# Two infini-attention and dense layers on one core: tile 3's statistics, tile 0's evacuation, the order of the first k and q products, and beta's load

## The chip, the cores and the metric

The kernel runs on one core of a Trainium2 chip. The engines of that core are TensorE (PE, matmuls, with PEld for its weight loads), VectorE (DVE), ScalarE (ACT), GpSimd (POOL) and SyncE (SP, which here only issues DMAs). The metric is the time of one execution in microseconds (us); less is better.

## The reference

A block of two layers is applied twice to a sequence `x` of 2048 tokens with 640 features, in bf16:

```python
x = x + _A_ref(_layernorm(x), wq, wk, wv, wo, beta)
x = x + _B_ref(_layernorm(x), w1, w2)      # relu(x @ w1) @ w2, 1728 hidden features
x = x + _A_ref(_layernorm(x), wq, wk, wv, wo, beta)
x = x + _B_ref(_layernorm(x), w1, w2)
```

The attention `_A_ref` has 32 heads of 20 features and cuts the sequence into four segments of 512 tokens. In each segment a causal softmax attention is computed within the segment, and a linear attention reads a memory `M` with a normaliser `z`; the two are mixed by a gate per head:

```python
g = _sigmoid(beta)
p = _softmax(q k^T * scale + mask)
o = g * (phi(q) M) / (phi(q) z + 1e-6) + (1 - g) * p v
M, z = M + phi(k)^T v, z + sum(phi(k))
```

## The kernel before

The sequence is held in SBUF as 16 tiles of 128 tokens (`x_sb`); a segment `s` is four tiles, and `a` (0 or 1) counts the applications of the attention. A segment goes through these stages: layer norm per tile and a transpose (`xnT`); q and k products, evacuated from PSUM to `stg`; v products; the heads' rows brought to partitions 0, 32, 64 and 96 in `pad` by DMA, since PE then computes four heads' scores side by side; scores (L1230); exponentials on ACT into `PT` (L1292); the causal mask on GpSimd (L1304); the products of `PT` and v (L1324, or L1363 for the first segment); division, gate, output projection, residual; layer norm; the two dense products; residual. Work of different segments overlaps.

**The planner.** The order on the engines isn't written by hand. Each stage is a Python generator, a *stream*, that yields one operation at a time. `Sched.run` keeps an estimated time for each engine and for each result, and repeatedly picks, among the streams' next operations, the one with the lowest key: its estimated start, plus a lateness term, plus a shift from the table `SHIFT`, with the stream's priority to break ties. The order that comes out is fixed in the program; on the chip each engine works its list in that order and waits on semaphores. The table's key is (number of the stream, rank), where the rank counts segments for most streams and is 0 throughout for those made by `items` and for `exps`. The streams that matter here, by number: 0 the scores, 1 `exps` (the exponentials), 21 `first_sums`, 22 to 25 `first_one(0)` to `first_one(3)`, 26 `first_ln_b`, 28 `proj_first`, 31 `proj_v`, 35 `warm_pe`, 36 `consts`, 37 `loads`.

The planner's estimates that the prediction uses: engines are free from 800 ns; an operation's result is seen after a tail (DVE 95, ACT 125, GpSimd 60, PE 190 ns) and 60 ns more for the semaphore, with 80 more on PE; a DVE operation of n elements takes 66 + n / (0.96 x mode) ns, one on ACT 60 (from PSUM) or 94 + n / 1.2; a DMA adds its bytes at 330 per ns to one common line and lands 1470 ns (x's first tiles) or 2000 ns later. A change between the layouts in which PE runs (full array, four column groups, row groups) is charged `SWITCH_NS`, 96 ns. An operation made by `evac` may run on ACT or DVE, whichever the planner sees done first.

**The start**, which the change edits. `loads` (L540 to L568) issues tiles 0 and 1 of x on SP, tiles 2 and 3 on ACT, then beta (64 bytes) on ACT, and on SP wk and wq in two pieces each (256 columns, then the rest), wv, and the next four tiles. `warm_pe` (L668) fills two small tiles and lets PE run 41 matmuls on a constant while nothing is loaded, and later multiplies beta by ones to spread it over the partitions. `consts` makes an identity matrix, constants and masks, and the gate from beta: an exponential on ACT (L646), DVE steps to L651, and the mask products at L658; `omg`, the gate's complement, is first used at L1377.

The first four tiles are normalised one by one. For tiles 0 and 1, `first_sums` has DVE compute the statistics (`stats`, two BATCH_NORM_STATS2 at L723 and an aggregate at L725), and `chain` has GpSimd compute 1 / sqrt(var + eps) in two steps (L733 or L737, then L739). For tiles 2 and 3, `first_ln_b` has ACT do the sums: a copy with a sum (L840), the mean (L842), a square with a sum (L844), and then the same two steps on GpSimd. `first_tile` normalises a tile on DVE (L781), transposes it by five matmuls with the identity (L794) and copies the result from PSUM to `xnT`: on DVE for tiles 0 and 1 (L803), on either engine for tiles 2 and 3 (L805).

`proj_first` then issues the first segment's q and k products in pieces: for tile 0, then tile 1, then tiles 2 and 3 together, each for the feature chunks c = 0 and 1 and for k (n = 0) and q (n = 1); then the chunks 2 to 4 for all four tiles at once. A piece is five matmuls of 128 x 128 by 128 or 256 tokens (L702) and one evacuation (L910 on DVE, L911 on ACT). A piece is planned only when the evacuation of the one before it has been planned. When the chunks 0 and 1 are done, `first_heads` (L1026) fetches the first heads' rows into `pad` by small DMAs, four on SP and the rest on ACT, and the first scores can run; the v products of the segment (L702, evacuated at L965) are planned once chunk 1's q is evacuated.

Of the kernel before, what the change touches and what calls it, by code (L numbers as in the profile page):

```python
# [10 lines left out]
D = 640  # L11
# [147 lines left out]
class Spawn:  # L159
# [12 lines left out]
PE_MARGIN = 80.0  # L172
HOLDERS = 1
SHIFT = {
    (5, 0): -3000, (7, 0): -700, (7, 1): 400, (7, 2): -1000, (7, 4): 4300, (7, 5): -1100, (7, 6): -2700,
    (8, 1): -200, (8, 4): -100, (8, 5): -100, (8, 6): -100, (8, 7): -400, (9, 3): -200, (9, 7): -300, (10, 1): -1400,
    (10, 4): 500, (10, 5): -100, (11, 1): -200, (11, 2): -100, (11, 3): -1500, (11, 4): 100, (11, 5): -1500,
    (11, 6): -3000, (12, 1): -200, (12, 2): 3400, (12, 3): 1500, (12, 4): 500, (12, 5): 1100, (12, 6): -200,
    (12, 7): 100, (13, 0): -500, (13, 1): -500, (13, 2): 1000, (13, 4): -400, (13, 5): 1400, (13, 6): 1500,
    (13, 7): 3000, (14, 1): 200, (14, 2): 300, (14, 3): -200, (14, 6): 300, (14, 7): 300, (15, 0): -400,  # L180
    (15, 2): 200, (15, 4): 400, (15, 6): 100, (16, 2): -200, (16, 5): 100, (16, 6): 300, (16, 7): 400, (17, 7): -300,
    (18, 1): -200, (18, 2): -100, (18, 3): -200, (18, 7): -400, (19, 0): -1600, (19, 1): 100, (19, 4): -100,
    (19, 5): -400, (19, 6): 1000, (20, 0): -200, (21, 0): 200, (22, 0): 100, (24, 0): 100, (26, 0): -100,
    (27, 4): 200, (27, 5): 200, (27, 6): -100, (27, 7): -100, (29, 6): -100, (29, 7): -400, (30, 6): -400,
    (31, 4): -400, (32, 7): 100, (33, 0): -500, (33, 1): -100, (33, 2): 200, (33, 3): 100, (33, 4): 400,
    (33, 5): -1400, (33, 7): -200, (34, 4): -800, (34, 7): -200, (36, 0): 100, (37, 0): 1500, (38, 0): -300,
}
HOLD_TOL = {"pe": 220.0, "act": 150.0, "dve": 200.0, "pool": 0.0, "sp": 0.0}

# [253 lines left out]
def bass_interleave_layers__memory_aug_infini_attn__dense_activation_relu__prompt_kernel(  # L443
    nc, A_x, A_wq, A_wk, A_wv, A_wo, A_beta, B_x, B_w1, B_w2, out,
):
    with contextlib.ExitStack() as es:
# [100 lines left out]
        def loads():  # L547
            def x_pair(name, t):
                yield from ld("sp", name, 327680, lambda e: e.dma_start(x_sb[:, t:t + 2, :], xs[:, t:t + 2, :]))

            def cols(name, w, src, c0, c1):
                yield from ld("sp", name, 1280 * (c1 - c0), lambda e: e.dma_start(
                    w[:, :, c0:c1], src.rearrange("(c p) d -> p c d", p=128)[:, :, c0:c1]))

            for t in range(4):
                yield from ld(("sp", "act")[t // 2], "x0%d%d" % divmod(t, 2), 163840, lambda e, t=t: e.dma_start(
                    x_sb[:, t, :], xs[:, t, :]))
            tz = yield Need("beta0")
            yield from ld("act", "beta", 64, lambda e: e.dma_start(
                beta_z[0:1, :], bass.AP(tensor=A_beta.tensor, offset=A_beta.offset, ap=[[H, 1], [1, H]])), tz)  # L560
            yield from cols("wk0", wk_r, A_wk, 0, 256)
            yield from cols("wq0", wq_r, A_wq, 0, 256)
            yield from cols("wk1", wk_r, A_wk, 256, D)
            yield from cols("wq1", wq_r, A_wq, 256, D)
            yield from wload("sp", "wv", wv_r, A_wv)
            yield from x_pair("x10", 4)
            yield from x_pair("x11", 6)

# [39 lines left out]

        def consts():
            tw = yield dve(4, 1, lambda e: e.memset(warm[:], 0.0))  # L610
            yield act(4, lambda e: e.activation(warm[:], warm[:], ACT.Exp), [tw], psum=False)
            t0 = yield pool(150, lambda e: e.memset(ident, 0.0))
            t1 = yield pool(250, lambda e: e.affine_select(
# [53 lines left out]

        def warm_pe():  # L668

            tw = yield dve(128, 1, lambda e: e.memset(warm_w, 1.0))  # L670
            tz = yield dve(32, 1, lambda e: e.memset(beta_z[:], 0.0))
            S.set("beta0", tks=[tz])
            yield Acq([X])
            tk = yield pe(107.0 * 41, [(warm_mm, k == 40) for k in range(41)], [tw])
            X.release(tk)
            tb = yield Need("beta")
            yield Need("first", 1)
            bk, tk = yield pe(40.0, [(lambda e, bk: e.matmul(
                bk.ap[:, 0:H], warm_w, beta_z[:], start=True, stop=True), True)], tb, acq=MISC)
            PTS[0].tks = [tk]  # L680
            S.set("betab", tks=[bk, tk])
# [47 lines left out]
        def chain(t0, n, tk, sq=None):  # L729

            sl = slice(t0, t0 + n)
            if n == 1 and sq is None:
                tk = yield pool(150, lambda e: e.tensor_scalar(lnU[:, sl], mv[:, sl, 1], 1.0, LN_EPS, ALU.mult, ALU.add), tk)  # L733
            elif sq is None:
                tk = yield dve(n, 1, lambda e: e.tensor_scalar(lnU[:, sl], mv[:, sl, 1], LN_EPS, None, ALU.add), tk, port=True)  # L735
            else:
                tk = yield pool(190, lambda e: e.tensor_scalar(lnU[:, sl], sq, 1.0 / D, LN_EPS, ALU.mult, ALU.add), tk)  # L737
            h = yield Need("mhalf")
            tk = yield pool(520 if n == 1 else 700, lambda e: e.tensor_tensor(rstd[:, sl], lnU[:, sl], mhalf[:, 0:n], ALU.pow), [tk] + h)  # L739
            return tk  # L740

        def turn(slot_sem, dst, src, waits):
# [42 lines left out]
        def first_tile(t, bx, tch):  # L785

            xt = yield Need("xts", 0, 0)
            xt = xt[0]
            k = t % 2
            tn = yield normed(t, k, bx, tch)  # L790
            S.set("normed", t, tks=[tn])
            idt = yield Need("ident")
            pb = lambda bk: bk.ap.bitcast(dt.bfloat16)
            fns = [(lambda e, bk, c=c: e.transpose(  # L794
                pb(bk)[:, c * 128:(c + 1) * 128], bx.ap[:, k * D + c * 128:k * D + c * 128 + 128], ident),
                c == FC - 1) for c in range(FC)]
            bk, tT = yield pe((85.0 if t == 0 else 56.0) * FC, fns, [tn] + idt, acq=MISC)
            if t == 0:
                yield pe(380.0, [(warm_mm, False) for _ in range(5)])
            dst = xt.ap[:, t * FC:(t + 1) * FC, :].rearrange("p c n -> p (c n)")  # L800
            src = pb(bk)[:, 0:D]
            if t < 2:
                tc = yield dve(D, 2, lambda e: e.tensor_copy(dst, src), [tT])  # L803
            else:
                tc = yield evac(D, 2, lambda e: e.tensor_copy(dst, src), lambda e: e.activation(dst, src, ACT.Copy), [tT])  # L805
            bk.release(tc)
            S.set("turned0", t, tks=[tc])
            FIRST.setdefault(t // 2, []).append((tc, tT))
            if len(FIRST[t // 2]) == 2:
                bx.release(*[x for _, x in FIRST[t // 2]])  # L810
                S.set("xt", 0, 0, t // 2, tks=[x for x, _ in FIRST[t // 2]])
# [4 lines left out]
        def first_sums():  # L816

            xt = yield Acq(XNT_A)
            xt.users = []
            S.set("xts", 0, 0, tks=[xt])  # L820
            bx = yield Acq(XN)
            S.set("bx", 0, tks=[bx])
            for t in range(2):
                w = yield Need("x00%d" % t)
                tk = yield from stats(t, w)
                tch = yield from chain(t, 1, [tk])
                S.set("first", t, tks=[tch])

        def first_one(t):
            bx = yield Need("bx", t // 2)  # L830
# [2 lines left out]

        def first_ln_b():
            junk = hT[:, 10:13, :].rearrange("p c n -> p (c n)")
            bx = None
            for t in (2, 3):
                w = yield Need("x01%d" % (t - 2))
                j = junk[:, (t - 2) * D:(t - 1) * D]
                tk = yield act(D + 130, lambda e, t=t, j=j: e.activation(  # L840
                    j, x_sb[:, t, :], ACT.Copy, accum_out=asum[:, t - 2:t - 1]), w, psum=False)
                tm = yield act(100, lambda e, t=t: e.activation(  # L842
                    mv[:, t, 0:1], asum[:, t - 2:t - 1], ACT.Copy, scale=1.0 / D), [tk], psum=False)
                tk = yield act(D + 250, lambda e, t=t, j=j: e.activation(  # L844
                    j, x_sb[:, t, :], ACT.Square, scale=-1.0, bias=mv[:, t, 0:1],
                    accum_out=asum[:, t:t + 1]), [tm], psum=False)
                yield Spawn(5, second(t, tk))

        def second(t, tk):
            tch = yield from chain(t, 1, [tk], sq=asum[:, t:t + 1])  # L850
            if t == 2:
                bx = yield Acq(XN)
                S.set("bx", 1, tks=[bx])
# [65 lines left out]
            return tk  # L919

        def proj_first():
            order = [(c, n, h) for h in range(len(PIECES)) for c in range(2) for n in range(2)]
            order += [(c, n, None) for c in range(2, FC) for n in range(2)]
            for z, (c, n, h) in enumerate(order):
                if z >= 1:
# [748 lines left out]
```

## Time and profile before

| | us |
|---|---|
| median of three timed runs | 555.7 (554.97 to 555.84) |
| profiled execution | 554.18 |
| its span on the profile page | 552.1 |
| PE busy in the span | 544.5 |
| DVE, ACT, GpSimd busy | 417.5, 413.0, 195.8 |

The granted clock of PE is 1.00 throughout. The span runs from the first instruction of the program to the end of the last; 2.1 us of the profiled execution lie around it. The page's rows of forty slices show the busy share of each engine in tenths (9 is 90% or more). The "chain that ended last" is followed back from the last instruction: at each step to what released it or to the instruction before it on its engine. A line of the timeline or of a group of instructions names the line of the kernel, the engine, the operation and its tiles (out <- in); in brackets stands how long the engine was idle before it and what ended that. PE's matmuls are pipelined, so the length of a line of PE holds some 0.2 us of drain after the last one; the start of the next line tells how long it held the engine.

### The profile page before, as it was taken

The numbers are of one execution on the slowest core, as the hardware profiler recorded it, in microseconds if no ns is written. First come the engines' busy times: TensorE is split into PE (matmuls) and PEld (weight loads), VectorE is DVE, ScalarE is ACT, GpSimd is POOL, SyncE is SP. The second block draws the span as 40 slices with busy tenths as digits, with TensorE's granted clock in tenths as the row PEclk, the third lists the DMA queues.
The fourth block names the chain that finished last, engine by engine and source line by source line (L and its number), as shares of the span: only waits on it lengthen the run. The fifth ranks groups of instructions, "written<-read, shape, count | busy, mean of one in ns | idle before, by whom it ended". The sixth has DMA issues, their size and how long they took to land.

```text
span 552.1 us, 22367 instructions
## 1 busy us (share of the span) xinstructions
PE 544.5 (99%) x9969; PEld 311.6 (56%) x9969; DVE 417.5 (76%) x1052; ACT 413.0 (75%) x531; POOL 195.8 (35%) x305
## 2 busy tenths in 40 slices
PE   8999999999999999999999999999999999999998
PEld 7554554455554555646456465654646654766656
DVE  4977899899798949987788759987968788745102
ACT  6699779889878878788888858888887779423140
POOL 5345334333344334443434404444333434201000
PEclk9999999999999999999999999999999999999999
DMA  8596989623861533953377841359138521433101
GB/s 266 147 224 179 195 202 209 195 78 66 170 146 44 78 68 100 151 98 69 62 143 151 136 147 45 69 97 136 23 103 174 93 50 29 96 63 62 40 2 51
DMA packets 130163, 61.52 MB, mean 111 GB/s; under 512 B 108948, under 2 KB 119956, under 8 KB 130068
## 3 DMA queue, kind: packets, MB, share of 16 engines
q1 hardware_dynamic: 129504, 59.57, 50.4%
q8 instruction: 78, 1.28, 0.9%
q10 hardware_dynamic: 564, 0.53, 0.4%
q14 instruction: 17, 0.14, 0.1%
HBM read 20.56 MB, written 12.85 MB: 61 GB/s over the span
## 4 chain that ended last, share of the span: by engine, by line
PE 88%; ACT 6%; DMA 2%; DVE 2%; SPq 1%; issue 0%
PE ps L705 43%; PE ps L702 27%; PE ps L1230 9%; PE ps L1324 6%; ACT PT L1292 5%; PE ps L1110 2%; DMA wq_r<-in_A_wq_dram 1%; PE ps L1504 1%; DMA pad<-scr 1%; PE ps L1167 1%; DMA pad<-stg 0%; ACT stg L1075 0%; SPq L1026 0%; DVE stats L723 0%; DVE o_sb L1418 0%
## 5 line engine op out<-in xcount | busy, mean ns | idle before, releaser
L1292 ACT ACTIVATE PT<-ps 128x1024 bf16<-128x1024 f32 x320 | 308.8, 1032 | 55.9 <-PE ps L1230 53.9
L1304 POOL TENSOR_SCALAR_AFFINE_SELECT PT<-PT 128x512 bf16<-128x512 bf16 x256 | 169.0, 678 | 250.2 <-ACT PT L1292 250.2
L705 PE MATMUL ps<-xnT,w_r 128*32 128x512 bf16 x1464 | 89.1, 380 | 0.0
L705 PE MATMUL ps<-w_r,hT 128*32 128x320 bf16 (+1 forms) x1868 | 71.2, 295 | 0.0
L1230 PE MATMUL ps<-pad 20*128 20x512 bf16 (+3 forms) x1024 | 63.4, 301 | 0.8 <-DMA pad<-scr 0.3
L1550 DVE TENSOR_TENSOR x_sb<-x_sb,ps 128x320 bf16<-128x320 bf16 (+1 forms) x65 | 30.9, 475 | 43.6 <-PE ps L705 39.9
L702 PE MATMUL ps<-w_r,hT 128*128 128x320 bf16 x378 | 62.4, 300 | 0.0
L723 DVE BATCH_NORM_STATS2 stats<-x_sb 128x6 f32<-128x320 bf16 x124 | 55.2, 478 | 3.2 <-DMA x_sb<-in_A_x_dram 2.6
L705 PEld LDWEIGHTS ps<-xnT,w_r 128*32 128x32 bf16 x1464 | 36.0, 97 | 33.6 <-issue 4.4
L705 PEld LDWEIGHTS ps<-w_r,hT 128*32 128x32 bf16 x1868 | 47.5, 97 | 12.7 <-issue 0.2
L1529 ACT ACTIVATE hT<-ps 128x512 bf16<-128x512 f32 x55 | 33.0, 599 | 21.1 <-PE ps L705 19.6
L1230 PEld LDWEIGHTS ps<-pad 20*128 20x128 bf16 x1024 | 17.9, 92 | 53.1 <-ACT PT L1292 26.9
L1446 DVE TENSOR_TENSOR x_sb<-x_sb,ps 128x320 bf16<-128x320 bf16 x64 | 30.5, 481 | 19.3 <-PE ps L705 15.1
L702 PEld LDWEIGHTS ps<-w_r,hT 128*128 128x128 bf16 x378 | 34.8, 98 | 18.2 <-issue 5.3
L1324 PE MATMUL ps<-PT,v_aug 128*21 128x128 bf16 (+3 forms) x896 | 40.3, 300 | 0.0
L910 DVE CAST stg<-ps 128x512 bf16<-128x512 f32 (+1 forms) x41 | 27.3, 668 | 16.6 <-PE ps L705 9.5
L739 POOL TENSOR_TENSOR rstd<-lnU,mhalf 128x2 f32<-128x2 f32 (+2 forms) x27 | 21.1, 781 | 50.9 <-DVE lnU L735 43.4
L1528 DVE TENSOR_SCALAR hT<-ps 128x512 bf16<-128x512 f32 x49 | 33.5, 685 | 7.3 <-PE ps L705 6.0
L702 PE MATMUL ps<-xnT,w_r 128*128 128x512 bf16 x154 | 37.4, 380 | 0.0
L705 PE MATMUL ps<-wo_r,oT 128*32 128x320 bf16 x864 | 36.7, 300 | 0.0
L1334 DVE CAST otu<-ps 128x512 bf16<-128x512 f32 x45 | 30.7, 682 | 5.5 <-PE ps L1324 4.2
L1075 ACT ACTIVATE stg<-stg 128x512 bf16<-128x512 bf16 x50 | 31.7, 636 | 1.2 <-DVE rtmp L1073 1.0
(114 smaller groups left out, 741.3 us busy)
## 6 DMA issues: line engine op xcount, KB each, us to landing
pad<-scr SPq DMA_DIRECT2D x124, 80.0 KB
scr<-stg SPq DMA_DIRECT2D x34, 256.0 KB, 2.8
out_dram<-x_sb SPq DMA_DIRECT2D x15, 160.0 KB, 2.8
w_r<-in_B_w_dram SPq DMA_DIRECT2D x10, 216.0 KB, 2.6
w_r<-in_B_w_dram SPq DMA_DIRECT2D x13, 160.0 KB, 2.8
x_sb<-in_A_x_dram SPq DMA_DIRECT2D x10, 160.0 KB, 3.0
scr<-w_r SPq DMA_DIRECT2D x5, 256.0 KB, 3.2
wv_r<-in_A_wv_dram SPq DMA_DIRECT2D x1, 800.0 KB, 9.7
```

The source lines that it names most:

```text
L702: return e.matmul(view(dst.ap, b), a, b, start=(k == 0), stop=(k == last))
L705: return e.matmul(view(dst.ap[rows], b), part, b, start=(k == 0), stop=(k == last))
L723: tk = yield dve(320, 1, lambda e, c2=c2: e.bn_stats(stats6[:, t, c2, :], x_sb[:, t, c2 * 320:(c2 + 1) * 320]), xt)
L1075: te = yield act(512, lambda e, q=q: e.activation(q, q, ACT.Exp), [tr] + p, psum=False)
L1230: fns.append([(lambda e, z=z, j=j, hh=hh, N=N, o=o, sl=sl, q=hh % 2: e.matmul(slot.ap[:, q, o:o + N], sl.ap[32 * hh:32 * hh + DH, z, 0, 12 ...
L1292: tx = yield act(1024, lambda e, dst=dst, src=src: e.activation(dst, src, ACT.Exp, scale=SCALE), sc + pw)
L1304: tm = yield pool(600.0, lambda e, reg=reg: e.affine_select(out=reg, in_=reg, pattern=[[0, 4], [1, 128]], compare_op=ALU.is_ge, fill=0.0, ...
L1324: fns.append((lambda e, OD, j=j, hh=hh: e.matmul(OD.ap[32 * hh:32 * hh + DH + 1, 128 * j:L], VAUG[vx(a, s)][:, j, 4 * g + hh, :], pt.ap[:, ...
L1334: te = yield evac(L, 1, lambda e: e.tensor_copy(dst, OD.ap), lambda e: e.activation(dst, OD.ap, ACT.Copy), [tk] + OTU[0].tks)
L1528: th = yield evac(512, 1, lambda e: e.tensor_scalar(hT[:, dc, :], bk.ap[:, :], 0.0, None, ALU.max), lambda e: e.activation(hT[:, dc, :], b ...
L1529: lambda e: e.activation(hT[:, dc, :], bk.ap[:, :], ACT.Relu), [tk] + HT.tks)
L1550: ta = yield dve(n, 1, lambda e: e.tensor_tensor(x_sb[:, t, c0:c0 + n], x_sb[:, t, c0:c0 + n], bk.ap[:, 0:n], ALU.add), [tk], urgent=True)
```

## The change

- Statistics of tile 3 move from ACT (`first_ln_b`) to DVE: `first_sums` now goes over the tiles 0, 1 and 3, and waits, for tile 3, until the normalisation of tile 0 has been planned. What follows the statistics runs as a stream of its own (`second`).
- Tile 0's transposes are evacuated by ACT.
- The normalisation of tile 2 is planned only after tile 1's evacuation.
- `proj_first` goes over tiles 0 and 1 with k ahead of q: k of tile 0, k of tile 1, q of tile 0, q of tile 1. Tiles 2 and 3 keep their order.
- beta is loaded on SP behind wv, not on ACT behind tile 3.
- `warm_pe` is planned after the memset of `warm`; `chain` has its two GpSimd branches merged into one.
- The table `SHIFT` is replaced as a whole (some eighty entries before and after). Among the new entries is one for all the exponentials, `(1, 0): -400`, and one for the causal masks, `(2, 0): 600`.

```diff
 SHIFT = {
-    (5, 0): -3000, (7, 0): -700, (7, 1): 400, (7, 2): -1000, (7, 4): 4300, (7, 5): -1100, (7, 6): -2700,
...
-    (33, 5): -1400, (33, 7): -200, (34, 4): -800, (34, 7): -200, (36, 0): 100, (37, 0): 1500, (38, 0): -300,
+    (1, 0): -400, (2, 0): 600, (5, 0): -700, (7, 0): -300, (7, 1): 100, (7, 6): -400, (8, 2): -400, (8, 3): 100,
...
+    (21, 0): -800, (23, 0): -400, (26, 0): 500, (27, 4): -200, (27, 5): -400, (27, 6): -100, (27, 7): -800,
...
+    (34, 7): 300, (36, 0): 100, (37, 0): 3000, (38, 0): 200,
 }
...
-            tz = yield Need("beta0")
-            yield from ld("act", "beta", 64, lambda e: e.dma_start(
-                beta_z[0:1, :], bass.AP(tensor=A_beta.tensor, offset=A_beta.offset, ap=[[H, 1], [1, H]])), tz)
             yield from cols("wk0", wk_r, A_wk, 0, 256)
...
             yield from wload("sp", "wv", wv_r, A_wv)
+            tz = yield Need("beta0")
+            yield from ld("sp", "beta", 64, lambda e: e.dma_start(
+                beta_z[0:1, :], bass.AP(tensor=A_beta.tensor, offset=A_beta.offset, ap=[[H, 1], [1, H]])), tz)
             yield from x_pair("x10", 4)
...
             tw = yield dve(4, 1, lambda e: e.memset(warm[:], 0.0))
+            S.set("warm")
...
         def warm_pe():
 
+            yield Need("warm")
             tw = yield dve(128, 1, lambda e: e.memset(warm_w, 1.0))
...
             k = t % 2
+            if t == 2:
+                yield Need("turned0", 1)
             tn = yield normed(t, k, bx, tch)
...
-            if t < 2:
+            if t == 0:
+                tc = yield act(D, lambda e: e.activation(dst, src, ACT.Copy), [tT])
+            elif t == 1:
                 tc = yield dve(D, 2, lambda e: e.tensor_copy(dst, src), [tT])
...
-            for t in range(2):
-                w = yield Need("x00%d" % t)
+            for t in (0, 1, 3):
+                w = yield Need("x0%d%d" % divmod(t, 2))
+                if t == 3:
+                    yield Need("normed", 0)
                 tk = yield from stats(t, w)
-                tch = yield from chain(t, 1, [tk])
-                S.set("first", t, tks=[tch])
+                yield Spawn(5, second(t, tk))
...
-            order = [(c, n, h) for h in range(len(PIECES)) for c in range(2) for n in range(2)]
+            order = [(c, n, h) for n in range(2) for h in range(2) for c in range(2)]
+            order += [(c, n, 2) for c in range(2) for n in range(2)]
             order += [(c, n, None) for c in range(2, FC) for n in range(2)]
```

## The prediction

> **What bounds the kernel.** I read the table of forty slices and the chain first, then TensorE by stages, then the first 20 us instruction by instruction.
>
> ```profile
> span 552.1 us, 22367 instructions
> PE   8999999999999999999999999999999999999998
> PE 88%; ACT 6%; DMA 2%; DVE 2%; SPq 1%; issue 0%
> ```
>
> TensorE (PE) is busy nearly everywhere, and 88% of the chain is its work. So a change can only win where PE waits, or where it makes PE's own work shorter. The table by stages shows where PE waits; after each span stand PE, PEld, DVE, ACT and POOL, busy us and instructions:
>
> ```profile
> 7.30:8.90 1.60, 0.48 (x7) 0.28 (x6) 1.05 (x3) 1.02 (x3) 0.37 (x2) 1.00 1.06 356
> 8.90:12.00 3.10, 2.96 (x46) 2.62 (x47) 1.23 (x3) 2.08 (x7) 2.35 (x6) 1.00 1.08 355
> 26.00:40.00 14.00, 13.60 (x204) 7.87 (x202) 11.20 (x28) 13.86 (x19) 6.33 (x10) 1.00 0.92 227
> 40.00:62.00 22.00, 20.33 (x305) 10.23 (x301) 16.86 (x49) 21.73 (x26) 13.23 (x20) 1.00 0.75 193
> 190.00:230.00 40.00, 40.00 (x664) 22.84 (x666) 31.28 (x83) 31.81 (x39) 14.89 (x22) 1.00 0.47 95
> ```
>
> PE idles 1.12 us in the second before 8.90, and 2.07 us between 26 and 62, where ScalarE (ACT) is 99% busy (35.59 of 36) and is the bound. From 190 on there is nothing to gain by waiting less. The opening, in the timeline (start, length):
>
> ```profile
> 6.34 0.74 ACT L840 ACTIVATE hT<-x_sb 128x640 bf16<-128x640 bf16 x1 [0.61 <-DMA x_sb<-in_A_x_dram]
> 6.43 0.45 DVE L781 TENSOR_SCALAR xn_tok<-x_sb,mv,rstd 128x640 bf16<-128x640 bf16 x1 [0.73 <-POOL rstd L739]
> 7.33 0.45 PE L702 MATMUL ps<-xnT,wk_r 128*128 128x128 bf16 x5
> 8.90 0.45 PE L702 MATMUL ps<-xnT,wq_r 128*128 128x128 bf16 x5 [1.12 <-DMA wq_r<-in_A_wq_dram]
> 11.90 0.72 PE L702 MATMUL ps<-xnT,wk_r 128*128 128x256 bf16 x5
> 14.21 0.84 PE L702 MATMUL ps<-wv_r,xnT 128*128 128x320 bf16 x5
> 18.70 0.40 PE L1230 MATMUL ps<-pad 20*128 20x512 bf16 x4
> ```
>
> One k product runs at 7.33, and then the queue stands until wq's first columns arrive. Tiles 2 and 3 enter at 11.90, wv's products at 14.21, the first scores at 18.70, and with them the exponentials that bound 26 to 62.
>
> **The start, step by step.** The planner fixes the order from its own estimates; on the chip each engine keeps that order and waits.
>
> *Tile 3.* ACT loses its five instructions for it (0.74 + 0.19 + 0.20 + 0.83 + 0.19 = 2.15 us, from 6.34 to 8.36); VectorE (DVE) gains two statistics and an aggregate (3.16 to 4.29 for tile 0, 1.13). From the planner's constants, x03 (tile 3's load) lands at 4.56 us, so it puts these three behind tile 0's normalisation (DVE free at 5.70) and, with the shift of -800 for `first_sums`, ahead of tile 1's. But the row at 6.34 says when x03 really landed. So DVE stands from 5.70 to 6.34 and ends the three at 7.47; tile 1 is normalised from 7.47 to 7.92, not from 6.43: 1.04 late. For tile 3, GpSimd's two (4.38 to 5.22 for tile 0, 0.84) then end near 8.4, against 9.27 now.
>
> *Tile 0's copy.* ACT did tile 2's in 0.70, DVE tile 0's in 0.56 but only from 6.79, behind tile 1's normalisation. On ACT, free by 5.73, it runs from about 6.5 to 7.2: 0.1 earlier than 7.33. This helps only if PE has nothing older to wait for, and it has: by the planner's times tile 1's transposes come at 7.28, the first k product at 7.39, so the transposes stand ahead in PE's queue. They go at 7.97 (0.05 after the normalisation, as now).
>
> *k ahead of q.* Five transposes or five 128-column matmuls take PE 0.28. Tile 1's transposes end at 8.25, tile 0's two k products at 8.81; tile 1's copy starts 0.49 after its transposes (10.86 to 11.35 for tile 3) and takes 0.49, to 8.95; its two k products run from 9.00 to 9.56. Tile 2 is normalised behind that copy, to 9.40, tile 3 to 9.85; their transposes run to 9.84 and from 9.90 to 10.18; four q products end at 11.30; tile 3's copy is done by 11.09 on ACT. So tiles 2 and 3 enter at 11.30 instead of 11.90: **0.6 us gained**. The ends: if x03 were early and tile 1 not late, all four k products would fit before 8.90, and from there only one set of transposes and four q products remain, 5 x 0.28 = 1.4: entry at 10.3, 1.6 gained. If the evacuations or the PSUM banks hold the row up as at 10.86 now (0.28 idle), nothing is gained.
>
> *Does it reach the end?* The four products of tiles 2 and 3 end 0.6 earlier, near 13.5, but wv lands at 14.1 (issued at 4.42, 9.7 to landing), and the planner, expecting it at 12.54, puts wv's products right there. PE loses most of its 0.6 again. The q and k of the first heads are out 0.6 earlier all the same; SP's four issues to `pad` (from 13.67) and the scores (18.70) follow, near 18.1, and ACT's chain with them. Between 26 and 62 ACT is the bound and PE has slack, so 0.6 of the chain is 0.6 at the end. If `pad` is held up, it is nothing.
>
> *beta.* ACT loses an issue of 0.54 at 2.08, hidden under its wait until 3.71: nothing. SP gets one behind wv's (ends 6.92); the two x loads behind it are issued 0.55 later but have 800 KB of wv ahead of them: nothing. The matmul of beta (now at 5.47) goes behind the products of tiles 2 and 3 in PE's queue; the gate chain on ACT and DVE is wanted first at 29.86 (`rden`), so 9 us late is covered. Now beta was used 3.4 us after its issue at 2.08; at that price it lands near 10.4, before it is wanted.
> The Trainium skill ("DMA: Bandwidth & Descriptors", section "Queues, rings and completion order") says instead that each DMA engine takes a ring's descriptors in order. By that rule beta comes behind its engine's share of wv, up to 14.1, and PE waits for it where it waits for wv anyway: the sum would stay.
>
> *Other edits.* The `warm` event reorders three memsets (0.17, 0.07 and 0.06) under ACT's table load of 1.28; GpSimd's merged branch for `lnU` is the same instruction. Nothing.
>
> **The new table of shifts.** It reorders everything after 20 us, and the trace can't show that. What is legible is `(1, 0): -400`: every exponential is planned 0.4 us earlier against the evacuations, which DVE can take too. What ACT did between 26 and 62:
>
> ```profile
> L1292 ACT ACTIVATE PT<-ps 128x1024 bf16<-128x1024 f32 x35 | 32.7, 1115 | 0.2
> L1075 ACT ACTIVATE stg<-stg 128x512 bf16<-128x512 bf16 x4 | 2.8, 697 | 0.0
> L965 ACT ACTIVATE v_aug<-ps 128x320 bf16<-128x320 f32 x2 | 0.9, 440 | 0.0
> L911 ACT ACTIVATE w_r<-ps 128x512 bf16<-128x512 f32 x1 | 0.8, 833 | 0.0
> L911 ACT ACTIVATE stg<-ps 128x512 bf16<-128x512 f32 x1 | 0.6, 627 | 0.0
> ```
>
> The last three (2.3 us) can leave ACT; L1075's exponentials can't. Ends: 2.3 gained if all go, and the same 2.3 lost if reordering moves as much onto it (DVE is full from 26 to 30). I take half, **1.2 us gained**, since the one legible entry points that way and DVE is 78% busy over the stretch.
>
> **Sum.** 0.6 + 1.2 = 1.8. The profiled execution took 554.18 (span 552.1 and 2.1 around it), so its like should take 552.4. The three timed runs have a median of 555.7, 1.5 above it; I forecast their kind: **553.9 us**. A measurement of this kernel tells about 0.2% (1.1 us) from no change, so faster means under 554.6 and slower over 556.8.
>
> **Rivals.**
> 1. *Both larger.* Tile 1 comes in time and ACT sheds all it can: 1.6 + 2.3 = 3.9, 551.8. Against it: the row at 6.34.
> 2. *Gated at 14.* wv, and beta behind it, hold PE to 14.1, the `pad` transfers stand behind the x loads in SP's ring, so the scores stay at 18.7, and what leaves ACT comes back as waits for DVE: 0 to 0.6 gained, 555.3. For it: the DMA engines are busy throughout from 7.3 to 12 (share 1.06 and 1.08). This is also the case that the k products don't fill the gap.
> 3. *Slower: more changes of tiling.* PE packs four matmuls side by side for scores and many projections, and changing between layouts costs:
>
> ```profile
> 131.56 0.39 PE L1230 MATMUL ps<-pad 20*128 20x512 bf16 x4
> 131.89 2.48 PE L702 MATMUL ps<-wv_r,xnT 128*128 128x320 bf16 x17
> 485.10 6.86 PE L705 MATMUL ps<-xnT,w_r 128*32 128x512 bf16 x124
> 491.79 5.61 PE L705 MATMUL ps<-wo_r,oT 128*32 128x320 bf16 x160
> ```
>
> Undisturbed, 31 sets of four take 6.69, 0.216 each; a lone score round with a change on either side takes 0.33. A pair of changes costs 0.115. After 62 us this is paid in full. There are about 160 score rounds; with 26 more pairs around them and the other packed groups, 3.0 us, the forecast's 1.8 is gone and it is slower by over 1.1; with 31, 3.6 us, it takes 557.5. For it: a table of some eighty entries replaced. Against it: the planner still charges each change 96 ns.
>
> **Chances.** Forecast 0.50 (own range 552.8 to 554.6), both larger 0.15, gated 0.20, slower 0.15. Faster 0.65, same 0.20, slower 0.15. The range, 551.5 to 556.8, takes in the first three but the far end of the second case.
>
> **What would show it.** Right: DVE waiting for x_sb near 5.7; tile 1's transposes near 8; two or more k products before the first q; tiles 2 and 3 near 11.3; scores near 18.1; fewer evacuations on ACT from 26 to 62. Wrong: tiles 2 and 3 before 10.5 (x03 early) or after 11.9; scores at 18.7 or later (gated); PE as full as now from 62 on with a later end (more changes of tiling).

## The result and the profile after

The changed kernel takes 559.47 us (median of 6, 558.0 to 560.94) where the kernel before took 555.34 beside it (6, 553.61 to 556.86): ratio 1.0078, 95% interval 1.0051 to 1.0105. It is slower; the forecast was 553.9, and 559.5 lies outside its range. The profiled execution took 560.47, its span is 558.2, 6.1 more than before.

The head of the page of the changed kernel and the shares of the chain:

```profile
span 558.2 us, 23218 instructions
...
PE 78%; DVE 12%; DMA 6%; ACT 2%; POOL 1%; issue 1%; SPq 0%
```

PE's busy time has hardly grown (545.2 for 544.5), so nearly all of the 6.1 is time in which PE stands. The chain, whose shares were 88% for PE before, points the same way: PE now has 78% of it, DVE 12% and DMA 6%. The stages, with the columns as in the prediction (PE, PEld, DVE, ACT, POOL, clock):

```profile
40.00:62.00 22.00, 18.60 (x288) 9.37 (x285) 17.76 (x46) 18.98 (x21) 11.29 (x18) 0.92 0.69 177
...
90.00:130.00 40.00, 38.77 (x812) 19.05 (x813) 33.49 (x85) 35.91 (x47) 15.74 (x24) 1.00 0.76 175
...
480.00:500.00 20.00, 18.94 (x520) 13.52 (x513) 13.11 (x36) 1.65 (x3) 1.53 (x2) 1.00 0.47 86
```

From 40 to 62 PE is less busy than before (18.60 for 20.33), and so is ACT (18.98 for 21.73); the clock's mean is 0.92 there, for 1.00 before. From 90 to 130 and from 480 to 500, where PE was never idle before (40.00 of 40 and 20.00 of 20), it now stands 1.23 and 1.06 us. The waits of PE from 70 us on (total us, times, longest) say for whom; for the kernel before the same view is empty:

```profile
PE ps L706 <- DMA oT<-o_sb: 1.1, 1, 1.1
PE ps L706 <- DVE x_sb L1451: 0.7, 1, 0.7
PE ps L706 <- DMA xnT<-xn_tok: 0.6, 1, 0.6
PE ps L1172 <- DMA phk<-phs: 0.6, 1, 0.6
PE ps L1115 <- DVE phs L1081: 0.5, 1, 0.5
```

They stand at 489, 391, 314, 120 and 98 us and are 3.6 us together (a sixth, of 0.2, is left out). (The line numbers are those of the changed kernel: L1235 are its scores, L1297 its exponentials, L703 and L706 its products.) The start, in the timeline:

```profile
5.81 0.45 DVE L782 TENSOR_SCALAR xn_tok<-x_sb,mv,rstd 128x640 bf16<-128x640 bf16 x1
...
6.17 0.88 DVE L724 BATCH_NORM_STATS2 stats<-x_sb 128x6 f32<-128x320 bf16 x2
...
7.21 0.39 DVE L782 TENSOR_SCALAR xn_tok<-x_sb,mv,rstd 128x640 bf16<-128x640 bf16 x1
...
7.95 1.20 PE L703 MATMUL ps<-xnT,wk_r 128*128 128x128 bf16 x15
...
11.76 0.71 PE L703 MATMUL ps<-xnT,wk_r 128*128 128x256 bf16 x5
...
18.07 0.39 PE L1235 MATMUL ps<-pad 20*128 20x512 bf16 x4
```

Tile 3's statistics run at 6.17, tile 1 is normalised behind them, three k products follow each other from 7.95, and the scores come at 18.07 instead of 18.70. So the start ended nearly where the forecast put it. But the row at 6.17 has no wait: DVE comes straight from tile 0's normalisation and doesn't stand for tile 3, as the forecast had it. The two groups of more than half a microsecond that ACT has left between 26 and 62 us:

```profile
L1297 ACT ACTIVATE PT<-ps 128x1024 bf16<-128x1024 f32 x33 | 30.9, 1042 | 3.7 <-PE ps L1235 3.6
L1080 ACT ACTIVATE stg<-stg 128x512 bf16<-128x512 bf16 x3 | 1.9, 632 | 0.0
```

The evacuations are all gone from ACT, as in the forecast's better case (L1080 are exponentials). But in the last column ACT now stands 3.7 us there, waiting for scores; before, that was 0.2. More idle time came back than the evacuations had taken.

### The profile page after: what moved, and what is told of

The parts are those of the page before. It is cut to its first block, busy times and chain, and to the rows that moved or that the text cites. A ratio compares the mean times of both kernels' runs of the same rounds, so it can differ in the third digit from the quotient of the medians.

```text
span 558.2 us, 23218 instructions
## 1 busy us (share of the span) xinstructions
PE 545.2 (98%) x10392; PEld 312.9 (56%) x10392; DVE 420.3 (75%) x1067; ACT 405.9 (73%) x514; POOL 195.9 (35%) x305
## 4 chain that ended last, share of the span: by engine, by line
PE 78%; DVE 12%; DMA 6%; ACT 2%; POOL 1%; issue 1%; SPq 0%
PE ps L706 39%; PE ps L703 23%; PE ps L1235 7%; PE ps L1329 5%; DMA oT<-o_sb 3%; DVE stats L724 2%; PE ps L1115 2%; ACT PT L1297 2%; DVE xn_tok L770 1%; DVE o_sb L1423 1%; DMA phk<-phs 1%; DMA xnT<-xn_tok 1%; DVE phs L1081 1%; DMA scr<-stg 1%; PE ps L1368 1%
## 5 line engine op out<-in xcount | busy, mean ns | idle before, releaser
L1297 ACT ACTIVATE PT<-ps 128x1024 bf16<-128x1024 f32 x320 | 309.2, 1025 | 61.7 <-PE ps L1235 59.8
L706 PE MATMUL ps<-xnT,w_r 128*32 128x512 bf16 x1828 | 114.0, 380 | 0.2 <-DVE hT L1533 0.2
L1534 ACT ACTIVATE hT<-ps 128x512 bf16<-128x512 f32 x56 | 33.4, 601 | 54.3 <-PE ps L706 53.1
L706 PE MATMUL ps<-w_r,hT 128*32 128x320 bf16 (+1 forms) x1936 | 72.5, 295 | 0.0
L706 PEld LDWEIGHTS ps<-xnT,w_r 128*32 128x32 bf16 x1828 | 45.3, 96 | 41.6 <-issue 4.8
L1235 PE MATMUL ps<-pad 20*128 20x512 bf16 (+3 forms) x1024 | 63.5, 301 | 0.9 <-ACT PT L1297 0.8
L703 PE MATMUL ps<-w_r,hT 128*128 128x320 bf16 x361 | 57.8, 300 | 0.0
L706 PEld LDWEIGHTS ps<-w_r,hT 128*32 128x32 bf16 x1936 | 50.0, 97 | 13.0
L1235 PEld LDWEIGHTS ps<-pad 20*128 20x128 bf16 x1024 | 17.9, 92 | 53.4 <-ACT PT L1297 27.5
L703 PEld LDWEIGHTS ps<-w_r,hT 128*128 128x128 bf16 x361 | 33.5, 98 | 17.6 <-issue 5.3
L740 POOL TENSOR_TENSOR rstd<-lnU,mhalf 128x2 f32<-128x2 f32 (+1 forms) x23 | 19.1, 828 | 58.9 <-DVE lnU L739 58.0
L914 DVE CAST stg<-ps 128x512 bf16<-128x512 f32 x46 | 31.2, 680 | 6.8 <-PE ps L706 6.3
L706 PE MATMUL ps<-wo_r,oT 128*32 128x320 bf16 x808 | 32.9, 300 | 2.0 <-DMA oT<-o_sb 1.1
L1423 DVE TENSOR_TENSOR o_sb<-otk,rden 128x320 bf16<-128x320 bf16 x56 | 32.2, 596 | 1.7 <-DMA oT<-o_sb 1.3
L770 DVE TENSOR_SCALAR xn_tok<-x_sb,mv,rstd 128x640 bf16<-128x640 bf16 x60 | 29.6, 534 | 4.6 <-POOL rstd L740 4.5
L1080 ACT ACTIVATE stg<-stg 128x512 bf16<-128x512 bf16 x50 | 31.7, 634 | 0.6 <-DVE rtmp L1078 0.5
```

The source lines that it names most:

```text
L703: return e.matmul(view(dst.ap, b), a, b, start=(k == 0), stop=(k == last))
L706: return e.matmul(view(dst.ap[rows], b), part, b, start=(k == 0), stop=(k == last))
L770: nm = lambda e, bx, t, k: e.tensor_scalar(bx.ap[:, k * D:k * D + D], x_sb[:, t + k, :], mv[:, t + k, 0:1], rstd[:, t + k:t + k + 1], ALU. ...
L1080: te = yield act(512, lambda e, q=q: e.activation(q, q, ACT.Exp), [tr] + p, psum=False)
L1235: fns.append([(lambda e, z=z, j=j, hh=hh, N=N, o=o, sl=sl, q=hh % 2: e.matmul(slot.ap[:, q, o:o + N], sl.ap[32 * hh:32 * hh + DH, z, 0, 12 ...
L1297: tx = yield act(1024, lambda e, dst=dst, src=src: e.activation(dst, src, ACT.Exp, scale=SCALE), sc + pw)
```

## The experiments

The theory: the order after 18 us loses the time, in places where PE waits for a transpose or for DVE, and the start doesn't. Its rivals: the start itself loses it; or one place, the wait of 1.76 us at 57 with the halved clock that follows, loses it all. For most runs the planner was given a recorded order instead of its own choice, so that two orders can be joined at a time of the plan, or single picks moved (a pick names the operation, its engine and PE's layout). The code for it is the same in all of them; what differs is the recorded list, and the diffs of picks below tell it in words. A letter names a theory, and means something else from one expectation to the next.

```diff
+            if self.order:
...
+                for z, (lab, i, k, m) in enumerate(self.order):
+                    if (lab, i) in can:
...
+                heads = []
```

"Work" below is what PE has streamed of its matmuls' columns up to a time, counted from the trace (four matmuls side by side once, 512 columns as 0.21 us), against the run with the new start and the old order.

**The new start with the old order.**

```diff
+ picks before 18 us: as the changed kernel's plan
  picks from 18 us: as the plan of before
```

> All edits of the change up to about 18 us, and from there on the order of the kernel before, pick by pick. Theory A (the loss is the new order after 18 us; the start itself gains): first scores near 18.1 as in the changed kernel, no wait of PE over 0.8 us after 20, no drop of the granted clock, and 0.6 to 1.0 us faster than before (ratio 0.998 to 0.999). Theory B (the new start upsets what follows: late beta, exponentials that arrive early, x loads behind beta): slower than before by 3 us or more, with a long wait of PE between 40 and 60 again.

554.09 for 554.45, ratio 0.9994 [0.9977, 1.0012]; span 551.6. The exponentials lead those of the kernel before by 0.64 us at 41 us, by 0.30 from 69 on, by 0.58 at the end. After 70 us no wait of PE is long enough to be listed. So the start isn't at fault; in this trace its gain is 0.3 to 0.6 us, and by the times it can't be told from no change.

**The old start with the new order.**

```diff
  picks before 18 us: as the plan of before
+ picks from 18 us: as the changed kernel's plan
```

> The kernel before up to about 18 us, and from there on the order of the changed kernel. Theory A: the loss stays and the start's gain goes: slower than before by 4 to 6 us (ratio 1.007 to 1.011), with PE's long wait between 52 and 58 and the dropped clock behind it. Theory B: within 1 us of before.

561.16 for 554.45, ratio 1.0118 [1.0086, 1.0149]. The order loses the time with either start. PE's wait at 57 us is only 0.24 here (1.76 in the changed kernel), and the loss is there all the same; one of the four executions had a mean clock of 1.00 and took 560.2.

**The wait at 57 taken away, and filled.** In the changed kernel PE stands longest here:

```profile
56.86 0.39 PE L703 MATMUL ps<-hT,wq_r 128*128 128x512 bf16 x1 [1.76 <-DVE o_sb L1385]
...
57.52 3.17 PE L703 MATMUL ps<-hT,wq_r 128*128 128x512 bf16 x7
```

DVE normalises the four tiles of a segment (L770, 1.10 for two, 0.35 and 0.82 us) between and ahead of the steps (L1381, L1382, L1385) that lead to the `o_sb` which frees PE's bank. Then the clock is halved: seven products of 512 columns take 3.17 us (the same seven take 1.69 at a clock of 1.00, in the run below with the new order up to 290 us). The first run moves the normalisation behind; the second leaves the order and gives PE eight products more to do, whose result nothing reads.

```diff
- division and o_sb of the head group between and behind the normalisations
+ division and o_sb ahead of them
```

> The changed kernel with one local change in VectorE's order near 54 us: the division of a head group (L1381, L1382, L1385) goes ahead of the normalisation of segment 2 that waited for GpSimd. Theory C (PE's wait of 1.76 us there cost twice, once as a wait and once by the clock that was halved for 3.41 us after it): both go, 2.5 to 3.5 us faster than the changed kernel, ratio to before 1.001 to 1.004. Rival D (only the wait itself counts, the slow stretch is hidden under ScalarE's exponentials): 1.8 us faster at most, ratio 1.004 to 1.006.

558.71 for 554.45, ratio 1.0074 [1.0052, 1.0095], slower than either theory had it. The wait is gone and PE is 1.3 us of work ahead of the changed kernel at 66 us; a wait of 1.31 us for `phk` at 120 (0.64 there) takes half of it back. The clock was halved in the profiled execution too, from 52.4. Its span is 556.4, but the changed kernel's six executions already lie between 555.7 and 558.6, so the times don't tell the two apart.

```diff
+            bk, tk = yield pe(1700.0, [... eight matmuls of 512 columns ...], acq=SC)
```

> The changed kernel with eight extra matmuls (128x512, results not used) on PE in the place where it waits near 55 us; the wait itself stays. Theory C: the clock stays at 1.00, and it is 1.2 to 1.9 us faster than the changed kernel, ratio to before 1.004 to 1.006. Rival D: the clock stays at 1.00 too, but the time is that of the changed kernel, ratio 1.007 to 1.009. If the clock drops all the same, idle time was not its cause.

558.94 for 554.45, ratio 1.0080 [1.0057, 1.0103]. In the profiled execution the clock was halved at 53.1 us, before the added products could keep PE busy. But the mean clock is kept of every execution: two of the four here had 1.00, no halved window, and took 557.93 and 559.0; so did one of the four above, 558.67. So the wait and the halved clock behind it are a small part of the loss at most.

**The new order up to 70 us alone, and from 70 us alone.**

```diff
  picks before 70 us: as the changed kernel's plan
- picks from 70 us:   as the changed kernel's plan
+ picks from 70 us:   as the run with the old order
```

> The changed kernel's order up to about 70 us, then the order of the kernel before. Theory E (the loss is made in several places; the first, between 42 and 66, costs about 1.2 us of PE's work against before and stays): 1 to 2 us slower than before, ratio 1.001 to 1.004, with a long wait of PE or a halved clock between 40 and 60. Rival F (nearly all is made in the first place, the rest follows from it): ratio 1.006 or more. Rival G (the first place is caught up later): ratio 0.999 to 1.001.

554.68 for 554.32, ratio 1.0001 [0.9974, 1.0027], although the profiled execution had waits of 0.79 and 0.65 us and a halved clock between 52 and 57. From 90 us on it is some 0.7 us of work behind and stays there.

```diff
- picks before 70 us: as the changed kernel's plan
+ picks before 70 us: as the run with the old order
  picks from 70 us:   as the changed kernel's plan
```

> The changed kernel's start to 18 us, the order of before to about 70 us, then the changed kernel's order. Theory E: the other places remain, 3 to 4.5 us slower than before, ratio 1.005 to 1.008, with waits of PE of half a microsecond or more near 98, 120, 315 and 489 us and no halved clock. Rival F: within 1 us of before.

559.36 for 554.32, ratio 1.0081 [1.0054, 1.0107], with the clock at 1.00 throughout (so in nine of its ten executions). This is the whole loss. It comes in steps: 1.0 us of work behind at 80, 1.8 at 100, 2.4 from 120 to 300, 3.7 at 320, 5.0 at 400, 6.0 from 490 on (the span is 5.7 longer; in the new order PE packs more of the `phk` products and has 0.4 us less to stream). The steps stand where PE waits (74 us: 0.70 for an exponential; 98: 0.53; 120: 0.36; 314: 0.57; 391: 0.71; 488: 0.60).

**The new order up to 290 us.**

```diff
  picks before 290 us: as the changed kernel's plan
- picks from 290 us:   as the changed kernel's plan
+ picks from 290 us:   as the run with the old order
```

> The changed kernel's order to 290 us, the old order of the picks from there. Theory F (losses add up by place): what is lost by 290 stays and nothing is added: the work curve stays 2.6 to 2.9 us behind, 557.1 or ratio 1.0045 to 1.005, and the waits at 314, 391 and 489 are not there. Rival (the whole order is at fault, or a late stretch waits on something set early): ratio 1.0075 to 1.008 as in the changed kernel, with waits past 290 again.

556.02 for 554.13, ratio 1.0020 [1.0001, 1.0039], less than expected. It is 1.5 us of work behind at 120 us and 1.9 at the end, and has no wait over 0.25 us past 119. The expected 2.6 to 2.9 was read from the changed kernel's profiled execution, whose clock was halved once; this profiled execution's stayed at 1.00. But nine of its twelve executions had a mean clock below 1.00, so why the median, too, is lower than expected stays open. By the ratios, some 0.6% of the changed kernel's 0.8% is made after 290 us, where PE was busy throughout before.

**Two late waits filled.** At 489 us PE stood for the transpose of `oT`, with a hundred products of the dense layer (w_r, hT; then xnT, w_r) ready behind it; at 314.8 it was the transpose of `xnT`. Nothing is added; picks change places:

```diff
- out projection of the last half segment (wo_r, oT), then 12 groups of (w_r, hT)
+ 12 groups of (w_r, hT), then the out projection
- v products of the next segment (wv_r, xnT), then 3 groups of (xnT, w_r)
+ 3 groups of (xnT, w_r), then the v products
```

> The changed kernel in its recorded order, with two moves: the twelve groups of the dense product (w_r, hT) that stood behind the last out projections stand ahead of them, where TensorE stood 1.06 us at 489 for the transpose of oT, and three groups of the dense product (xnT, w_r) stand ahead of the v products that waited 0.64 us at 314.8 for the transpose of xnT. No work is added or left out. Theory F (the late waits are losses in full, since TensorE is the bound there): both waits gone, 1.7 us back, 557.7 where the changed kernel has 559.4, ratio 1.005 against before. Theory G (what is filled in one place is lost in the next, as it was at 55 us): no gain, ratio 1.0075 to 1.008, and new waits behind the moved groups.

557.7 for 554.13, ratio 1.0054 [1.0033, 1.0074], what was expected if these waits are lost in full. The interval overlaps that of the changed kernel (1.0051 to 1.0105), so the traces have to tell. The place at 489 in the changed kernel, and then in this one, where L919 is the same line:

```profile
489.14 2.22 PE L706 MATMUL ps<-wo_r,oT 128*32 128x320 bf16 x60 [1.06 <-DMA oT<-o_sb]
```

```profile
485.43 2.21 PE L919 MATMUL ps<-wo_r,oT 128*32 128x320 bf16 x60
487.47 1.67 PE L919 MATMUL ps<-w_r,hT 128*32 128x320 bf16 x44
...
489.10 3.57 PE L919 MATMUL ps<-wo_r,oT 128*32 128x320 bf16 x100
```

The dense products run in the hole, the out projections behind them find `oT` landed, and no wait takes its place: PE is busy 20.00 of 20 us from 480 to 500. From 290 to 330 it is 40.00 of 40 (39.36 in the changed kernel). The span is 556.5, 1.7 below the changed kernel's 558.2, and the two waits were 0.64 + 1.06 = 1.70; that the two agree so well is luck, since this execution had one halved window more, lacks the wait at 391 (so do three of the runs above, which didn't touch it) and has two waits of 0.3 that the changed kernel's lacks. A firmer count is PE's busy time in the 210 us from 290 to 500: 209.06 here, 207.28 to 208.32 in the five traces that keep the changed kernel's order there, 210.00 in the old order. Filling the two places gave back 0.7 to 1.8 us of the 1.7 to 2.7 that PE idles there.

The rows also show that the view understates a wait. The 60 out projections at 485.43 are 2.21 us long (as long as the 60 ahead of the hole in the changed kernel), but the next group starts 2.04 after them; the rest is drain, which counts as busy where nothing follows. So a wait costs about 0.2 us more than its listed length.

**The evacuations off ACT, in the old order.** The second term of the forecast by itself:

```diff
  as the run with the new start and the old order
- evacuations between 24 and 62 us: on DVE or ACT
+ evacuations between 24 and 62 us: on DVE
```

> The new start with the old order, but the four evacuations that ScalarE makes between 26 and 62 us are made by VectorE in the same places. By the prediction's second term: 1.2 us faster than x3 (half of 2.3), exponentials earlier by as much at 60 us, ratio 0.997 to 0.998. Theory H (VectorE is what releases PE's banks there, and PE has to wait for it instead): exponentials not earlier at 70 us, 0 to 2 us slower than x3, ratio 0.999 to 1.003.

554.63, ratio 0.9997 [0.9971, 1.0024]; span 552.7 for 551.6. ACT between 26 and 62 us, here and then in the run with the new start and the old order:

```profile
L1510 ACT ACTIVATE PT<-ps 128x1024 bf16<-128x1024 f32 x34 | 31.5, 1147 | 1.0 <-PE ps L1448 0.8
```

```profile
L1510 ACT ACTIVATE PT<-ps 128x1024 bf16<-128x1024 f32 x34 | 31.5, 1164 | 0.1
...
L1183 ACT ACTIVATE v_aug<-ps 128x320 bf16<-128x320 f32 x2 | 1.2, 578 | 0.0
L1128 ACT ACTIVATE w_r<-ps 128x512 bf16<-128x512 f32 x1 | 0.9, 917 | 0.0
```

34 exponentials in the same stretch either way: they come 0.1 us later from 41 to 55 us, 0.33 later from 60, 0.9 from 166, 1.2 at the end. ACT was full, but nothing was waiting for the time it lost to evacuations: relieved of them, it waits 0.8 us for scores and then, at 62.46, 2.10 for a step of DVE's (0.33 with the evacuations on ACT). Two of the four evacuations couldn't have held up an exponential of the scores at all. In the kernel before they stand here:

```profile
60.47 0.83 ACT L911 ACTIVATE w_r<-ps 128x512 bf16<-128x512 f32 x1
61.33 0.44 ACT L965 ACTIVATE v_aug<-ps 128x320 bf16<-128x320 f32 x1
...
69.30 1.02 ACT L1292 ACTIVATE PT<-ps 128x1024 bf16<-128x1024 f32 x1 [0.41 <-PE ps L1230]
```

The last such exponential ahead of them starts at 59.05, and the next one, at 69.30, waits for its scores.

**Which part of the start.** The first run normalises tile 1 ahead of tile 3's statistics; the second has tile 3's statistics on DVE as its only edit to the kernel before.

```diff
  as the run with the new start and the old order
- normalisation of tile 1 behind the statistics of tile 3
+ normalisation of tile 1 ahead of them
```

> The new start with the old order (as the run x3), but on VectorE tile 1's normalisation goes ahead of tile 3's statistics, which wait for a load that lands at 6.3 us. If that wait is what held the start back: tile 1's transposes near 7.0 instead of 7.5, tiles 2 and 3 enter 0.3 to 0.6 us earlier than in x3, first scores near 17.7. Rival: the loads of wq (8.9) and wv (14.1) hold it, first scores within 0.2 us of x3's. Either way at most 0.5 us on the whole, ratio 0.997 to 1.000.

554.9 for 554.32, ratio 1.0013 [0.9978, 1.0048]. My expectation was wrong: the scores come 0.9 us later (18.82 for 17.92). PE waits 0.68 and 0.64 us for the normalisations of the later tiles, at 9.74 and 10.93: they are the gate, not tile 1. Nor did DVE stand for tile 3's load, as the expectation took for granted: it landed at 4.80 here.

```diff
-            for t in range(2):
+            for t in (0, 1, 3):
...
-            for t in (2, 3):
+            for t in (2,):
```

> The kernel before with tile 3's statistics on VectorE as the only edit; the picks after 18 us in the old order. If these statistics are what brings the first scores forward (the gate was tile 3, as the run with tile 1 ahead suggests): first scores at 18.0 to 18.2, tiles 2 and 3 entering near 11.3 to 11.8. If it is the four k products ahead of the q products: first scores at 18.5 to 18.7 and no gain. Its time, about 554, can't tell either from no change.

Tiles 2 and 3 enter at 11.34, but the scores only come at 18.37, which lies between the two expectations: there PE waits for `pad` (0.28), with one q product more ahead. So in this one execution the statistics bring 0.33 of the start's gain; the rest, to 17.92, needs the other edits. Its time, 553.79, can't be told from no change.

**The new code with the old table, planned anew.**

```diff
-    (1, 0): -400, (2, 0): 600, (5, 0): -700, (7, 0): -300, ...
+    (5, 0): -3000, (7, 0): -700, (7, 1): 400, (7, 2): -1000, ...
```

> The changed kernel with the table SHIFT of before, planned anew: the edits of the start alone, and whatever order the planner makes of them. Theory T (a table fits only the start that it was found with: a small move of the start changes the picks all along): far slower than both, ratio 1.015 to 1.035, with many more waits of TensorE after 70 us. Rival U (the old table is the better one, whatever the start): 554, ratio 0.998 to 1.002, as with the new start and the old order of picks.

578.11 for 554.13, ratio 1.0422 [1.0383, 1.0462], beyond the expected. Its start is as good as the changed kernel's, and then the scores stop:

```profile
18.06 0.39 PE L1236 MATMUL ps<-pad 20*128 20x512 bf16 x4
...
59.49 0.40 PE L1236 MATMUL ps<-pad 20*128 20x384 bf16 x8
...
84.95 0.40 PE L1236 MATMUL ps<-pad 20*128 20x512 bf16 x4
```

The last scores of the first segment stand at 59.49, the next segment's at 84.95; PE runs out projections and q, k and v products in between, and the exponentials pause for 24.6 us (10.2 in the kernel before). The clock is halved for 10.2 us from 30.8 and for 6.8 from 181. So the old table, which gives 555.3 with the old code, is 24 us worse than that with the new one: these shifts are fitted to their code, and the old table isn't good by itself. The new table with the old code was not tried.

## Why the prediction was wrong, point by point

- *What bounds the kernel* held, and I didn't carry it to its end. "From 190 on there is nothing to gain by waiting less" is right, but where nothing can be gained by waiting less, a wait that a new order brings is lost. The two filled waits bear it out, with 0.7 to 1.8 us of PE's time given back for waits of 1.2 to 1.8 in the traces that keep them.
- *The start, 0.6.* Near in nearly all its times: tile 3's statistics at 6.17 on DVE (forecast 6.34), tile 1 normalised at 7.21 (7.47), its transposes at 7.67 (7.97), k products behind them, tiles 2 and 3 at 11.76 (11.30; PE waited 0.56 us at 10.2 for the last normalisation, which the walk didn't have), scores at 18.07 (18.1). It stands in part at the end: with the old order the lead is 0.3 to 0.6 us, and 0.36 in the medians, within the noise.
  Part of this is luck. The walk took tile 3 to land at 6.3, as before, and DVE to stand for it from 5.7, the first sign of being right; neither happened. Tile 3 landed at 5.02, 3.6 us after its issue (4.7 before). But tile 0, with which DVE begins, landed at 3.69 (3.13 before), so DVE wasn't free for tile 3 until after 6, and the two misses about cancel. All eleven traces with the new start show both (3.4 to 3.6 us for tile 3; tile 0 at 3.42 to 3.69), the three with the old start's loads neither (4.2 to 4.7; 3.13 to 3.18). beta's load, which stood behind tile 3 on ACT, may be the reason for the first; its move alone was not tried, and the second has no reason on record.
- *beta.* Its matmul ran at 13.39 without a wait, ahead of wv's products at 13.97, so the move cost nothing, as forecast. The load landed at 12.18, 6 us after its issue at 6.23 and not 3.4; wv's landed at 12.97. So it came near the end of wv's load, the second of the two ways in the prediction. That its move may have brought tile 3 earlier wasn't in the sum.
- *The new table, 1.2.* **This step failed.** The forecast read one entry, `(1, 0): -400`, found the evacuations that could leave ACT, and took half of them as the worth of the whole table. They did leave ACT, all of them, and it was worth nothing: taken off by themselves, they made the exponentials 0.1 to 1.2 us later. That ACT is busy 99% of a stretch doesn't say that the end waits for it: 1.27 of the 2.3 us stood behind the last exponential of the segment, and for the rest the scores didn't come sooner. What the other entries do, the sum counted as zero. With the new code they make an order that costs about 5 us past 70 us (559.36 for 554.32), in places that the forecast hadn't looked at.
- *What the table does to waits.* The planner lets a product follow a transpose as closely as its constants allow: 1.4 us of issue and 2.4 more until the result is there (L747 of the changed kernel), 3.8. The median from issue to landing was 3.8 us before for `xnT`, `oT` and `phk` alike; after, it is 4.3, 4.0 and 4.6, and the `oT` for which PE waited 1.06 us took 5.0. In the old order no wait is listed at the places in question, so it had room there; the new one hasn't. Why the transposes take longer after was not tried, and two of the five waits are for DVE, which this doesn't explain.
- *Rival 3, slower by more changes of tiling.* The side was right and the mechanism wrong: there are 323 changes between layouts after and 326 before. Its chance of 0.15 was all that the forecast left for slower; no rival was a new order that lets PE wait in its full stretches. The second term's downside was set at 2.3 us, the price of ACT's evacuations, where that of a whole table can be as large as the 24 us that the old one costs on the new code.
- *What stays open.* Past 70 us the listed waits of the changed kernel sum to 3.6 us and its work falls behind by some 5. By estimate, five drains of 0.2 and the idle times too short for the view (0.6; PE idles 4.2 us in all past 70) make up the rest. Only two of the five places were filled; that the other three are losses of the same kind is argued from the steps of the work, not tried.

## What to carry to other kernels

Where an engine is never idle, don't ask of a new order what it can gain there; ask whether each long-latency result (a transposing DMA above all) still has as much independent work ahead of its user as before, and if not, put ready work there. A full engine is a bound only if something waits for it: look at what stands behind the work that you would take away, or take it away first and see who waits. And don't read the sign of a table of tuned constants from one entry; it was fitted to one code, so judge code and table together, or count the table as an unknown that is as large as what it controls.

## What the runs showed of the hardware

The granted clock fell to one half for one window of 3.41 us in the changed kernel, from 57.44 us. PE from 54.03 to 57.44 and from there to 60.85, busy time and clock:

```profile
54.03:57.44 3.41, 1.65 (x16) 0.43 (x15) 3.41 (x9) 2.56 (x3) 2.31 (x5) 1.00 0.87 190
57.44:60.85 3.41, 3.41 (x15) 1.02 (x15) 2.69 (x8) 1.94 (x2) 1.08 (x2) 0.50 0.58 110
```

In the window before, PE was busy 1.65 us of 3.41, and its longest wait there was 1.76 us. The same order up to 290 us had different fates in three profiled executions: one halved window in the changed kernel, two (6.8 us from 54.78) with the late waits filled, and none, with waits of 0.96 and 1.35 us at the same places, in the run that goes back to the old order at 290. At 70 us these stand 1.5 behind, 2.0 behind and 0.3 ahead of the old order in work, so there a halved window cost some 1.8 us. In the run with the new order up to 70 us it fell from 52.64 to 56.05, where PE had waited in the others, and that run stands 0.1 ahead at 70: the price depends on what PE had to do.

The old kernel has it too. Of the 70 timed executions of the kernel before that stand beside the runs, 56 had a mean clock of 1.00 (median 554.11) and 12 had 0.997, which is one such window (555.93): 1.8 us as well. In the changed kernel all six had one or two.

What PE streamed ahead of a drop can be counted. In each trace the windows of 3.413 us follow one another from the first change of the clock. In the eight windows that were followed by a drop, PE streamed 0.58 to 1.43 us of its columns; of all other windows at a clock of 1.00, in 14 traces, two had less than 1.43 (1.39 and 1.42, with the old start and the new order). "Busy" tells them apart less well: up to 2.62 of 3.41 us ahead of a drop. The counts fit a limit of about 1.4 us; that is an estimate, and no run was made to test it.

The Trainium skill ("TensorE: Matmul & The Clock Gate", section "HAM oscillation — how this bites in real kernels") names idle gaps over some 3.4 us as what drops the clock. Here it dropped with no gap longer than 1.76 us, and in the kernel with late waits filled with none over 1.09 ahead of it; the measurement decides, and so long a gap isn't needed.
